# A gated scan and a top-1 mixture of experts: loads in another order, two pages with an unsplit second layer, other planning numbers

## The chip, the cores and the metric

The kernel runs on one core of one Trainium2 chip. The metric is the device time of one launch in microseconds, the median of several runs; lower is better.

## The reference

A gated linear scan along the sequence (batch 4, length 5056, width 256) gives `y`. The 20224 vectors of `y` are the tokens of a mixture of 8 experts of which each token uses one.

```python
log_a = c * sig_r * np.log(np.clip(a_base, 1e-06, 1.0 - 1e-06))   # c = 8, sig_r, sig_i: sigmoids of the gates
a_t = np.exp(log_a)
norm = np.sqrt(np.maximum(1.0 - a_t * a_t, 1e-06))
x_gated = norm * sig_i * x
for t in range(S):
    h = a_t[:, t] * h + x_gated[:, t]
    y[:, t] = h
...
logits = x @ w_gate + modality_bias[modality_id]        # x is y as 20224 x 256; 2 modalities, 8 experts
e_idx = np.argmax(logits, axis=1)
gate_w = probs[np.arange(N), e_idx]                     # softmax of the logits
for e in range(E):
    h = np.maximum(x[mask] @ w1[e], 0.0)                # mask: tokens of expert e; w1 256 x 1024
    out[mask] = gate_w[mask, None] * (h @ w2[e])        # w2 1024 x 256
```

With these inputs all but 49 tokens go to two experts (10124 and 10051 tokens).

## The kernel before

**Stages.** The sequence is cut into 23 chunks (`CHUNKS`): four of 128 time steps, seventeen of 256, one of 128 and one of 64, each for all four batches, so that a chunk has 512 or 1024 tokens. For each chunk: `load_chunk` brings `a` (the r gate), `g` (the i gate) and `x` by the queue of SyncE (SP); `scan_chunk` makes the gates on ScalarE (ACT) and VectorE (DVE) and the scan itself on DVE (L567); `size_chunk` finds a power of two for scaling; `split_chunk` writes `y` as a pair of half-precision numbers, high and low, over `a` (ACT L698, DVE L701), and TensorE (PE) makes the logits from it (L714). `route_chunk` (DVE L775 to L851, PE L816 to L819) gives each token its place in its expert's list (`di`) and moves the running totals of the experts on. `rows_part` transposes `a` into token rows `rt` (SP, L739, one transpose for 128 tokens), and GpSimd (POOL) scatters them, 128 rows at a time, into `rows` in HBM, sorted by expert (L874).

**Pages.** The sorted rows are worked off in pages of 256 tokens, in turn for the two hot experts (`HOT = 2`); later pages have 512 tokens ("wide"), and a few small pages hold the rest and the cold experts. `choose_pages` picks two pages at a time from the running totals of the chunks routed so far (`sel`, on DVE). There are two forms of this choice. For early pages, those chosen from the first `EARLY` chunks (`last`), places of the page that aren't filled yet are masked (`had`; POOL makes `hadm` and `ids` at L1167 and L1171 for the output's scatter), and a page takes whatever tokens there are. Otherwise a margin (`behind`) is kept. `load_rows` reads a page transposed from `rows` (`X`, SP, L1194) with its ids and gates (`mt`, L1195). `first_layer` multiplies X by w1 (PE L1272, 48 products for 256 tokens), `relu_pair` writes H as a high and a low half (ACT L1207, DVE L1209), `second_layer` multiplies H by w2 (PE L1432, 48 products), `layer2_tail` applies the gate (ACT L1221), and POOL scatters the result to the output (L1227). PE mixes the first layer of a page with the second layer of the page before.

**Products in half precision.** The weights of the two hot experts are loaded as fp32 (`wr0` and `wr1`: w1 and w2 of the first, `wr2` and `wr3` of the second), scaled (`scale_of`: PE L334 and L341, DVE L337), and converted into a high half (ACT L364) and a low half (DVE L370), in two steps of 1024 columns each (`hw0_0`, `hw0_1`, `hw1_0`, `hw1_1`). Every product is then three half-precision products: high by high, high by low, low by high. Between them `iv` and `hiv` carry the scales that are undone in the gate factor `gt`.

**The order of the work.** Every stage is a generator that yields an engine, a planned duration and a condition. A planner inside the kernel (`run`) takes, again and again, the one that can start first by its planned times; among those of the same engine within `WINDOW` of it, the one with the better priority (`PRIO`, four numbers for each chunk: routing, split, scan, rows; `W_AT` for the weights). `PLAN` holds its durations and due times. Thus these tables set the order in which instructions stand on each engine, and nothing else: what really waits for what on the chip is settled by semaphores. Each engine and each queue works in its order, so an instruction that waits holds up all that stand behind it. `START` is the order of the first loads; `HURRY` says for how many chunks the planner picks by a wider window; `WAIT` says how long PE may be planned to stand idle for a page before the rest of the second layer of the page before is issued alone:

```python
if queue and (prev is None or ready_at(queue[0]) < free["PE"] + WAIT):
    cur = queue.pop(0)
```

Of the kernel before, what the change touches and what calls it, by code (L numbers as in the profile page):

```python
# [17 lines left out]
P = 128  # L18
# [12 lines left out]
CHUNKS = [(128 * k, 128) for k in range(4)] + [(512 + 256 * k, 256) for k in range(17)] + [(4864, 128), (4992, 64)]  # L31
# [5 lines left out]
WAIT = 4.0  # L37
WINDOW = 0.1
# [50 lines left out]
def kernel(  # L89
# [296 lines left out]
    loads, seq = [], 0  # L386
    for what in START.split():
        if what == "w":
            what, seq = f"w{seq}", seq + 1
        loads.append(what)  # L390
    assert seq == 2 * HOT
# [12 lines left out]

    def hot_weights(m):

        e, w = m // 2, m % 2
        yield "DMA", 2.9, allof(seen(("turn", loads.index(f"w{m}") - 1)), room("wr"), lambda: 8.4), -9.0
# [91 lines left out]
    def load_chunk(c):  # L500
# [10 lines left out]
        for i, (name, src) in enumerate((("a", rs), ("g", gs), ("x", xs))):  # L511
            tag = "H" if c == 0 and name != "g" else name
            yield "DMA", 2.9 * z, room(tag), -9.0
            tickets[c, name] = tag, take(tag)
            t = (pm if tag == "H" else pa).tile([P, cols], F32, name=f"{name}{c}", tag=tag, bufs=BUFS[tag])
            LOADS.dma_start(t, src[:, base : base + cols])
            got.append(t)
# [4 lines left out]
        mark["load", c] = plan["end"]  # L522
# [877 lines left out]
    def second_layer(prev, units):  # L1400

        pg, st = prev.pg, prev.pg.st
        while units:
# [24 lines left out]
            wv = (pg.w if pg.e is None else hw[pg.e])[1].rearrange("p (s f d) -> p s f d", s=2, f=NF)  # L1428
            for _, f in run_:
                for m, (hx, wx) in enumerate(((0, 0), (0, 1), (1, 0))):  # L1430
                    prev.count += 1
                    ins = nc.tensor.matmul(  # L1432
                        prev.po, prev.h(hx, f, rs_), wv[:, wx, f], start=(prev.count == 1), stop=(prev.count == 3 * NF)
                    )
            count["pe"] = ins.ins.name
            if prev.count == 3 * NF:
# [133 lines left out]
```

## Time and profile before

| what | value |
|---|---|
| runs | 956.75, 959.58, 956.82 us; median 956.82 |
| the profiled execution | 951.06 us, span 949.1 |
| granted TensorE clock, mean | 0.983 |
| busy share of PE, DVE, ACT, POOL | 92%, 73%, 70%, 54% |
| moved by DMA | 160.95 MB, 170 GB/s over the span |
| scatters of rows (L874) and of outputs (L1227) on POOL | 158 and 160 |

Times in the profile count from the start of its span. PE is TensorE's products, PEld its weight loads (beside the products), DVE VectorE, ACT ScalarE, POOL GpSimd, SP SyncE and SPq its queue of transfers. In a row of a timeline stand the start, the duration, the engine, line and operation, the tiles written and read, the count, and in brackets how long the engine was idle before and what ended that. In a row by stretches stand the stretch, its length, the busy time and the instruction count of PE, PEld, DVE, ACT and POOL, then the granted clock of PE, the share of the transfer engines and GB/s. In a row of a group stand form, count, busy time and the mean of one in ns.

### The profile page before, as it was taken

To read this page: it belongs to the slowest core of one execution; us is meant where nothing else is said; L and a number is where in the kernel's file an instruction comes from. 1 tells how busy PE (TensorE), PEld (TensorE's weight loads), DVE (VectorE), ACT (ScalarE), POOL (GpSimd) and SP (SyncE) were. 2 spreads that over 40 slices of the span, in tenths; PEclk is the share of its full clock that TensorE was granted. 3 is DMA by queue.
4 is the path that set the end of the run, shared out by engine and by line. 5 is a ranking of instruction groups with operands and counts; after the bars stand their busy time and mean duration, and the time that the engine had idled before them with its cause. 6 is when DMAs were issued, how large, how long until landed. Compare 5 with 4: busy or idle time off the path is not lost. (4 is left out here: it accounts for less than half of the span.)

```text
span 949.1 us, 22324 instructions
## 1 busy us (share of the span) xinstructions
PE 868.8 (92%) x8485; PEld 773.5 (81%) x8485; DVE 692.1 (73%) x1526; ACT 660.2 (70%) x942; POOL 516.6 (54%) x563
## 2 busy tenths in 40 slices
PE   2286599999979999999999999999999999999996
PEld 1275578888868888888888888888888888889896
DVE  5975876877977879877788888978786667653251
ACT  7967668969967889766988879844665555554342
POOL 6424756778886868776467677755454222212212
PEclk9997899999989999999999999999999999999999
DMA  8864788878768897699698988785642222212410
GB/s 284 256 189 102 204 205 232 260 182 207 219 227 242 188 229 234 144 271 244 178 285 202 277 175 217 156 172 120 180 106 79 51 51 58 62 46 57 131 35 26
DMA packets 223334, 160.95 MB, mean 170 GB/s; under 512 B 197359, under 2 KB 202097, under 8 KB 216690
## 3 DMA queue, kind: packets, MB, share of 16 engines
q1 hardware_dynamic: 206290, 115.02, 50.2%
q0 software_dynamic: 16224, 44.25, 14.4%
q8 instruction: 68, 1.11, 0.5%
q14 instruction: 48, 0.39, 0.1%
q10 hardware_dynamic: 704, 0.18, 0.1%
HBM read 72.96 MB, written 45.01 MB: 124 GB/s over the span
## 5 line engine op out<-in xcount | busy, mean ns | idle before, releaser
L1272 PE MATMUL ph<-X,hw 128*128 128x256 f16 (+1 forms) x2880 | 355.5, 274 | 26.9 <-DMA X<-rows 24.7
L1432 PE MATMUL po<-hw,H 128*128 128x256 f16 x2832 | 349.4, 272 | 3.6 <-issue 2.1
L1272 PEld LDWEIGHTS <-hw 128*128 128x128 f16 x2880 | 277.3, 99 | 62.7 <-issue 16.2
L1432 PEld LDWEIGHTS <-H 128*128 128x128 f16 x2880 | 277.1, 98 | 36.6 <-issue 3.3
L1227 POOL DMA_INDIRECT out_dram<-ot,mt x128 | 163.9, 1281 | 218.0 <-ACT ot L1221 184.7
L874 POOL DMA_INDIRECT rows<-rt,di x158 | 208.4, 1319 | 120.8 <-issue 30.4
L1209 DVE SCALAR_TENSOR_TENSOR H<-ph,H 128x512 f16<-128x512 f32 (+1 forms) x248 | 161.6, 667 | 105.3 <-ACT H L1207 89.6
L1207 ACT ACTIVATE H<-ph 128x512 f16<-128x512 f32 (+1 forms) x248 | 141.8, 577 | 122.3 <-PE ph L1272 103.5
L1221 ACT ACTIVATE ot<-po,gt 128x256 f32<-128x256 f32 x160 | 75.2, 470 | 45.7 <-PE po L1432 35.9
L567 DVE TENSOR_TENSOR_SCAN x<-a,x 128x2048 f32<-128x2048 f32 (+2 forms) x23 | 87.9, 3821 | 0.8
L1432 PE MATMUL po<-hw,Hx 128*128 128x256 f16 x480 | 68.4, 273 | 1.2 <-ACT ot L1221 0.7
L1432 PE MATMUL po<-hw,Hg 128*128 128x256 f16 x480 | 66.9, 273 | 0.0
L1227 POOL DMA_INDIRECT out_dram<-ot,ids x32 | 54.0, 1688 | 12.6 <-issue 4.9
L553 DVE TENSOR_TENSOR x<-g,x 128x2048 f32<-128x2048 f32 (+2 forms) x23 | 45.9, 1996 | 14.0 <-ACT x L551 12.0
L701 DVE SCALAR_TENSOR_TENSOR a<-x,scy,a 128x1024 f16<-128x1024 f32 (+2 forms) x46 | 50.9, 1128 | 3.1 <-ACT a L698 3.0
L698 ACT ACTIVATE a<-x,scy 128x1024 f16<-128x1024 f32 (+2 forms) x46 | 46.0, 1020 | 9.3 <-DVE scy L306 9.0
L1432 PEld LDWEIGHTS <-Hx 128*128 128x128 f16 x480 | 46.8, 98 | 6.8 <-issue 1.5
L1362 PEld LDWEIGHTS <-sw 128*128 128x128 f16 x480 | 47.0, 98 | 5.4
L1432 PEld LDWEIGHTS <-Hg 128*128 128x128 f16 x480 | 47.0, 98 | 5.4
L544 ACT ACTIVATE a<-a,ch 128x1024 f32<-128x1024 f32 (+2 forms) x46 | 50.5, 1115 | 0.1
L539 DVE SCALAR_TENSOR_TENSOR g<-g,x 128x2048 f32<-128x2048 f32 (+2 forms) x23 | 45.7, 1988 | 2.8 <-ACT g L535 2.8
L535 ACT ACTIVATE g<-g 128x2048 f32<-128x2048 f32 (+2 forms) x23 | 38.4, 1668 | 6.9 <-DMA g<-in_i_gate_dram 6.7
(224 smaller groups left out, 1090.6 us busy)
## 6 DMA issues: line engine op xcount, KB each, us to landing
a<-in_r_gate_dram SPq DMA_DIRECT2D x17, 1024.0 KB
g<-in_i_gate_dram SPq DMA_DIRECT2D x17, 1024.0 KB
x<-in_x_dram SPq DMA_DIRECT2D x17, 1024.0 KB
wr<-in_moe_w_dram SPq DMA_DIRECT2D x4, 1024.0 KB
cr<-in_moe_w_dram SPq DMA_DIRECT2D x4, 1024.0 KB
a<-in_r_gate_dram SPq DMA_DIRECT2D x5, 512.0 KB
g<-in_i_gate_dram SPq DMA_DIRECT2D x5, 512.0 KB
x<-in_x_dram SPq DMA_DIRECT2D x5, 512.0 KB
```

What stands on the lines that cost most here:

```text
L544: nc.scalar.activation(sl, sl, AF.Exp, scale=ch[:, h : h + 1], bias=ch[:, h : h + 1])
L567: nc.vector.tensor_tensor_scan(out=y, data0=a, data1=y, initial=0.0, op0=ALU.mult, op1=ALU.add)
L698: nc.scalar.activation(ys[:, 0, :, u, :], yg[:, :, u, :], AF.Copy, scale=sc)
L701: nc.vector.scalar_tensor_tensor(out=ys[:, 1, :, u, :], in0=yg[:, :, u, :], scalar=sc, in1=ys[:, 0, :, u, :], op0=ALU.mult, op1=ALU.subtract,)
L874: ins = nc.gpsimd.indirect_dma_start(out=rows[:, :], out_offset=bass.IndirectOffsetOnAxis(ap=idx, axis=0), in_=src, in_offset=None, bounds ...
L1207: nc.scalar.activation(hi, src, AF.Relu)
L1209: nc.vector.scalar_tensor_tensor(out=lo, in0=src, scalar=0.0, in1=hi, op0=ALU.max, op1=ALU.subtract)
L1221: nc.scalar.activation(ot, po, AF.Copy, scale=t.gt[:, a : a + 1])
L1227: ins = nc.gpsimd.indirect_dma_start(out=out[:, :], out_offset=bass.IndirectOffsetOnAxis(ap=t.mt[:, a, 0:1] if t.ids is None else t.ids[:, ...
L1272: ins = nc.tensor.matmul(ph[:, v, 0:st], lhsT, rhs, start=(m == 0 and v == 0), stop=(m == len(mm) - 1), skip_group_check=True,)
L1362: ins = nc.tensor.matmul(to[:, v, :], lhsT[s], rhs[x], start=(i in (1, 7) and v == 0 and m == 0), stop=(m == 2), skip_group_check=True,)
L1432: ins = nc.tensor.matmul(prev.po, prev.h(hx, f, rs_), wv[:, wx, f], start=(prev.count == 1), stop=(prev.count == 3 * NF))
```

## The change

1. The first loads come in another order: chunk 1 before the second weight, chunk 2 before the third and fourth. (w0 to w3 are the four weight transfers.)
2. Pages 0 and 1 (`WHOLE = 2`, one page of each hot expert) keep H as one fp32 tile, written by one relu on whichever of ACT and DVE the planner has free, and their second layer is 16 fp32 products by the raw w2 of 128 tokens (32 for a page, in place of 96). The raw w2 is therefore given back only after that page, and the gate factor undoes the scale of w1 alone.
3. `EARLY` 6 to 7: pages chosen from the first seven chunks take the masked form.
4. Other numbers for the planner: `WAIT` 4 to 3, `WINDOW` 0.1 to 0.05, `HURRY` 5 to 7, `W_AT`, `PRIO` for chunks 0 to 8, and transfer and due times in `PLAN` (`dma`, `l4`, `land`, w0 to w3, `xland`, and more). `CHUNKS` has the same values as before; it is written in another way.

```diff
-START = "0 w w 1 w w 2"
+START = "0 w0 1 w1 2 w2 w3"
+WHOLE = 2
-WAIT = 4.0
-WINDOW = 0.1
+WAIT = 3.0
+WINDOW = 0.05
-W_AT = [2, 2, 6, 3]
+W_AT = [2, 2, 4, 4]
-PRIO.update({0: (6, 1, 1, 1), 1: (22, 5, 6, 9), 2: (13, 29, 20, 14), 
...
+PRIO.update({0: (1, 1, 1, 1), 1: (5, 5, 6, 1), 2: (13, 24, 15, 14), 
...
-HURRY = 5
-EARLY = 6
+HURRY = 7
+EARLY = 7
-PLAN = dict(exact=12, w0=1, w1=4, w2=8, w3=4, xland=3, row=1.55, beside=7, op=0.2, gprio=3, oh=0.3, lag=1.5, latefrom=6, 
...
+PLAN = dict(dma=3.6, l4=24, exact=12, w0=6, w1=4, w2=4, w3=3, land=0.5, xland=1.0, row=1.55, beside=9, op=0.2, gprio=3, oh=0.15, lag=1, latefrom=8, 
...
@@ hot_weights(m): e, w = m // 2, m % 2
+        raw2[e, w] = raw, tr
...
-        give("wr", tr)
+        if w == 0:
+            give("wr", tr)
         if w == 1:
...
+            yield "SP", 0.0, seen(("raw", e)), 0.0
+            give("wr", tr)
@@ layer1_tail
+        if t.whole:
+            if free["ACT"] <= free["DVE"]:
+                nc.scalar.activation(t.H[:, hs, :], ph[:, :, 0:st], AF.Relu)
+            else:
+                nc.vector.tensor_scalar(out=t.H[:, hs, :], in0=ph[:, :, 0:st], scalar1=0.0, scalar2=None, op0=ALU.max)
+            give("ph", tp)
+            return
@@ second_layer
-                    conds.append(seen(("hot", pg.e)))
+                    conds.append(seen(("got", 2 * pg.e + 1), ("w", 2 * pg.e)) if prev.whole else seen(("hot", pg.e)))
...
+            if prev.whole:
+                wv, terms = raw2[pg.e, 1][0].rearrange("p (o f d) -> p o f d", o=1, f=NF), ((0, 0),)
+            else:
+                wv = (pg.w if pg.e is None else hw[pg.e])[1].rearrange("p (s f d) -> p s f d", s=2, f=NF)
+                terms = (0, 0), (0, 1), (1, 0)
@@ expert_layers
+                cur.whole = cur.pg.n < WHOLE
```

How the order moves is seen at three places. In the names, the number after a letter is the chunk's (`a1`, `rt1`, `g5`) or the page's (`X0`, `mt0`); lines after the change are some lines further on (L519 for L516, L742 for L739, L1197 for L1194, L877 for L874, L372 for L370, L570 for L567, L1170 for L1167).

The first is the start of the pages. SP before, from chunk 3's loads to the transposes of chunk 1:

```order
L516 DMA a3_567<-in_r_gate_dram 128x1024
L516 DMA g3_598<-in_i_gate_dram 128x1024
L516 DMA x3_605<-in_x_dram 128x1024
L1189 TENSOR_LOAD sel1_613
L1189 ISA x2
L1194 ISA
L1194 DMA_TRANSPOSE X0_0_634<-rows_78 128x4x256
L1195 ISA
L1195 DMA mt0_633<-rows_78 128x2x2
```

SP after, from the same loads:

```order
L519 DMA a3_558<-in_r_gate_dram 128x1024
L519 DMA g3_583<-in_i_gate_dram 128x1024
L742 DMA_TRANSPOSE rt1_0_604<-a1_294 128x4x128 x4
L1192 TENSOR_LOAD sel1_590
L1192 ISA x2
L1197 ISA
L1197 DMA_TRANSPOSE X0_0_687<-rows_78 128x4x256
L1198 ISA
L1198 DMA mt0_686<-rows_78 128x2x2
L519 DMA x3_705<-in_x_dram 128x1024
```

The four transposes of chunk 1 have moved from behind X1 (the next page) to ahead of X0, and chunk 3's x from ahead of X0 to behind it. On DVE at the same place, ahead of chunk 1's scan, before:

```order
L370 SCALAR_TENSOR_TENSOR hw0_1_219<-wr1_294,sc1_356,hw0_1_219 128x1024
L370 SCALAR_TENSOR_TENSOR hw1_1_221<-wr3_380,sc3_455,hw1_1_221 128x1024
L424 TENSOR_TENSOR hiv0_222<-iv0_311,iv1_357 128x1
L302 TENSOR_SCALAR hsc1_225<-pt2_489 128x1
L553 TENSOR_TENSOR x1_337<-g1_331,x1_337 128x1024
L306 TENSOR_SCALAR hsc1_225<-hsc1_225 128x1
L561 TENSOR_TENSOR fed1_587<-a1_308,last0_402 128x8
L308 TENSOR_SCALAR iv2_487<-hsc1_225 128x1
L563 TENSOR_TENSOR x1_337<-x1_337,fed1_587 128x8
L370 SCALAR_TENSOR_TENSOR hw1_1_221<-wr3_380,sc3_455,hw1_1_221 128x1024
L565 MEMSET a1_308 128x8
L567 SCALAR_TENSOR_TENSOR x1_337<-a1_308,x1_337 128x1024
```

and after:

```order
L556 TENSOR_TENSOR x1_302<-g1_297,x1_302 128x1024
L308 TENSOR_SCALAR sc1_384<-sc1_384 128x1
L868 TENSOR_SCALAR sg0_497<-sg0_497,scy0_355 128x4
L870 RECIPROCAL sg0_497<-sg0_497 128x4
L564 TENSOR_TENSOR fed1_505<-a1_294,last0_358 128x8
L310 TENSOR_SCALAR iv1_385<-sc1_384 128x1
L566 TENSOR_TENSOR x1_302<-x1_302,fed1_505 128x8
L568 MEMSET a1_294 128x8
L372 SCALAR_TENSOR_TENSOR hw0_0_218<-wr0_268,hsc0_224,hw0_0_218 128x1024
L570 SCALAR_TENSOR_TENSOR x1_302<-a1_294,x1_302 128x1024
```

The weights of the second hot expert (`hw1_1`, from `wr3`) no longer stand ahead of the scan of chunk 1.

The second place is SP from chunk 4's first transposes on. Before, from there to page 7's choice:

```order
L739 DMA_TRANSPOSE rt4_0_1587<-a4_793 128x8x128 x2
L1189 TENSOR_LOAD sel4_1606
L1189 ISA x2
L1194 ISA
L1194 DMA_TRANSPOSE X6_0_1683<-rows_78 128x4x256
L1195 ISA
L1195 DMA mt6_1682<-rows_78 128x2x2
L739 DMA_TRANSPOSE rt4_0_1587<-a4_793 128x8x128 x2
L1189 TENSOR_LOAD sel4_1606
```

and after, from chunk 4's last transpose ahead of chunk 7's loads to page 8:

```order
L742 DMA_TRANSPOSE rt4_0_1702<-a4_770 128x8x128
L519 DMA a7_1939<-in_r_gate_dram 128x2048
L519 DMA g7_1992<-in_i_gate_dram 128x2048
L519 DMA x7_2056<-in_x_dram 128x2048
L742 DMA_TRANSPOSE rt5_0_2156<-a5_1056 128x8x128
L1192 TENSOR_LOAD sel5_2120
L1192 ISA x2
L1197 ISA
L1197 DMA_TRANSPOSE X8_0_2226<-rows_78 128x4x256
```

X6 stands behind two transposes of chunk 4 in both; X8 stood behind two transposes of chunk 5 before and now stands behind one.

The third place is POOL, the scatters of chunk 4's rows. Before:

```order
L752 IOTA rt4_0_1587 128x8
L758 COPY rt4_0_1587<-sg4_1745 128x8
L874 DMA rows_78<-rt4_0_1587,di4_1765 166400x258 x2
L1167 TENSOR_SCALAR hadm4_1843<-slot_195,had4_1518 128x2
L874 DMA rows_78<-rt4_0_1587,di4_1765 166400x258
L1171 TENSOR_TENSOR ids4_1842<-hadm4_1843,mt4_1531 128x2
L1227 DMA out_0_dram<-ot4_0_1729,ids4_1842 20224x256
L874 DMA rows_78<-rt4_0_1587,di4_1765 166400x258
L1227 DMA out_0_dram<-ot4_0_1729,ids4_1842 20224x256
L874 DMA rows_78<-rt4_0_1587,di4_1765 166400x258 x3
L1167 TENSOR_SCALAR hadm5_2009<-slot_195,had4_1518 128x2
L874 DMA rows_78<-rt4_0_1587,di4_1765 166400x258
```

and after:

```order
L1170 TENSOR_SCALAR hadm5_1863<-slot_195,had4_1227 128x2
L755 IOTA rt4_0_1702 128x8
L761 COPY rt4_0_1702<-sg4_1752 128x8
L877 DMA rows_78<-rt4_0_1702,di4_1793 166400x258 x8
L1174 TENSOR_TENSOR ids5_1862<-hadm5_1863,mt5_1321 128x2
L1240 DMA out_0_dram<-ot5_0_1760,ids5_1862 20224x256 x2
```

Page 4's outputs, which stood among the scatters of chunk 4, now stand ahead of them, and page 5's behind.

On PE, the second layer of a page is issued alone, with no first layer mixed in, after pages 1, 3 and 17 in the order before, and after pages 5 and 7 in the order after. All pages, products and transfers are the same in number, but for those named in points 2 and 3.

More of the change, by code (lines that the diff above doesn't have):

```diff
@@ L29 @@
 TWO23 = float(1 << 23)
-CHUNKS = [(128 * k, 128) for k in range(4)] + [(512 + 256 * k, 256) for k in range(17)] + [(4864, 128), (4992, 64)]
+RUNS = [128] * 4 + [256] * 17 + [128, 64]
+CHUNKS = [(sum(RUNS[:k]), t) for k, t in enumerate(RUNS)]
 BUFS = {
@@ L383, in convert @@
             give("dg", td)
[L386 to L391, printed above, removed]
+    loads = START.split()
     mark["turn", -1] = 0.0
@@ L403 @@
     FACTOR = (1.0, 1.0 / 1024)
+    raw2 = {}
     def hot_weights(m):
         e, w = m // 2, m % 2
-        yield "DMA", 2.9, allof(seen(("turn", loads.index(f"w{m}") - 1)), room("wr"), lambda: 8.4), -9.0
+        yield "DMA", PLAN["dma"], allof(seen(("turn", loads.index(f"w{m}") - 1)), room("wr"), lambda: 8.4), -9.0
         tr = take("wr")
@@ L512, in load_chunk @@
             tag = "H" if c == 0 and name != "g" else name
-            yield "DMA", 2.9 * z, room(tag), -9.0
+            yield "DMA", (PLAN["dma"] if c < 9 else 2.9) * z, allof(room(tag), lambda: PLAN.get(f"l{c}", 0.0)), -9.0
             tickets[c, name] = tag, take(tag)
@@ L521, in load_chunk @@
         tiles[c] = got
-        mark["load", c] = plan["end"]
+        mark["load", c] = plan["end"] + PLAN["land"]
     def done(c, name):
@@ L1413, in second_layer @@
                 if pg.e is not None and not prev.to:
-                    conds.append(seen(("hot", pg.e)))
-            yield "PE", 0.328 * len(run_), allof(*conds), 0.0
+                    conds.append(seen(("got", 2 * pg.e + 1), ("w", 2 * pg.e)) if prev.whole else seen(("hot", pg.e)))
+            yield "PE", (0.45 if prev.whole else 0.328) * len(run_), allof(*conds), 0.0
             if not prev.to:
@@ L1418, in second_layer @@
                 prev.gt = sm.tile([P, st // P], F32, name=f"gt{prev.n}", tag="gt", bufs=3)
-                nc.vector.tensor_scalar(out=prev.gt, in0=gates, scalar1=pg.inv if pg.e is None else hiv[pg.e], scalar2=None, op0=ALU.mult)
+                nc.vector.tensor_scalar(out=prev.gt, in0=gates, scalar1=pg.inv if pg.e is None else tiles["wiv", 2 * pg.e] if prev.whole else hiv[pg.e], scalar2=None, op0=ALU.mult)
             if begins:
@@ L1427, in second_layer @@
             rs_ = slice(a * P, (a + 1) * P)
-            wv = (pg.w if pg.e is None else hw[pg.e])[1].rearrange("p (s f d) -> p s f d", s=2, f=NF)
+            if prev.whole:
+                wv, terms = raw2[pg.e, 1][0].rearrange("p (o f d) -> p o f d", o=1, f=NF), ((0, 0),)
+            else:
+                wv = (pg.w if pg.e is None else hw[pg.e])[1].rearrange("p (s f d) -> p s f d", s=2, f=NF)
+                terms = (0, 0), (0, 1), (1, 0)
+            products = len(terms) * NF
             for _, f in run_:
-                for m, (hx, wx) in enumerate(((0, 0), (0, 1), (1, 0))):
+                for hx, wx in terms:
                     prev.count += 1
                     ins = nc.tensor.matmul(
-                        prev.po, prev.h(hx, f, rs_), wv[:, wx, f], start=(prev.count == 1), stop=(prev.count == 3 * NF)
+                        prev.po, prev.h(hx, f, rs_), wv[:, wx, f], start=(prev.count == 1), stop=(prev.count == products)
                     )
             count["pe"] = ins.ins.name
-            if prev.count == 3 * NF:
+            if prev.whole and prev.count == products and a == st // P - 1 and prev.pg.n >= WHOLE - HOT:
+                mark["raw", pg.e] = plan["end"]
+            if prev.count == products:
                 prev.ended[a // 2] = prev.ended.get(a // 2, 0) + 1
```

16 lines of the change are left out of this document (11 added, 5 removed).

## The prediction

> **What bounds the kernel now.** I read the page's busy times first, then the busy time of each engine by stretches, and then the tensor engine's timeline at the stretches in which it stands idle.
>
> ```profile
> span 949.1 us, 22324 instructions
> PE 868.8 (92%) x8485; PEld 773.5 (81%) x8485; DVE 692.1 (73%) x1526; ACT 660.2 (70%) x942; POOL 516.6 (54%) x563
> ...
> 51.30:76.50 25.20, 23.34 (x215) 20.04 (x214) 19.05 (x53) 16.07 (x29) 9.95 (x8) 1.00 0.54 178
> 76.50:82.80 6.30, 0.00 (x0) 0.00 (x0) 3.65 (x3) 5.87 (x5) 5.16 (x7) 0.61 0.44 113
> 82.80:107.10 24.30, 24.26 (x216) 20.77 (x217) 16.70 (x52) 15.69 (x23) 8.09 (x11) 0.89 0.81 210
> 107.10:116.80 9.70, 0.00 (x0) 0.00 (x0) 8.61 (x15) 7.50 (x6) 8.98 (x6) 0.75 0.27 66
> 116.80:162.00 45.20, 41.77 (x409) 36.08 (x409) 30.87 (x74) 29.81 (x38) 29.50 (x36) 0.94 0.86 228
> 162.00:275.90 113.90, 113.31 (x1126) 101.28 (x1124) 95.97 (x196) 97.97 (x124) 87.19 (x78) 1.00 0.81 223
> 275.90:282.00 6.10, 0.27 (x9) 0.17 (x7) 2.39 (x2) 3.67 (x3) 5.19 (x6) 0.77 0.52 136
> 282.00:600.00 318.00, 315.82 (x3174) 282.04 (x3175) 260.56 (x542) 256.75 (x334) 221.26 (x199) 0.99 0.88 220
> 600.00:941.70 341.70, 337.43 (x3232) 302.49 (x3230) 215.92 (x481) 184.42 (x334) 114.31 (x117) 1.00 0.37 89
> ```
>
> After the length of each stretch stands PE's busy time; the granted clock is third from the end. The tensor engine bounds the kernel once expert pages run: from 162 on it is busy nearly throughout. It has nothing to do for pages before 51.3, and it is empty three times, 6.3, 9.7 and 6.1 us, each time at a granted clock of 0.61 to 0.77. The change touches work from the first load to about 290 us; the order of the rest only shifts.
>
> ```profile
> 51.32 6.67 PE L1272 MATMUL ph<-X,hw 128*128 128x256 f16 x48 [2.82 <-DMA X<-rows]
> 82.83 7.96 PE L1272 MATMUL ph<-X,hw 128*128 128x256 f16 x48 [6.36 <-DMA X<-rows]
> 116.81 2.72 PE L1272 MATMUL ph<-X,hw 128*128 128x256 f16 x12 [9.72 <-DMA X<-rows]
> 160.67 1.47 PE L1432 MATMUL po<-hw,H 128*128 128x256 f16 x12
> 161.98 1.47 PE L1272 MATMUL ph<-X,hw 128*128 128x256 f16 x12
> 282.02 2.74 PE L1272 MATMUL ph<-X,hw 128*128 128x256 f16 x12 [5.85 <-DMA X<-rows]
> 284.81 2.06 PE L1272 MATMUL ph<-X,hw 128*128 128x256 f16 x12
> ```
>
> Each wait ends with a transposed page (X) that comes late: pages 0, 2, 4 and 18. At full clock twelve products take 161.98 − 160.67 = 1.31 us, 0.109 each, so a layer of a 256-token page is 5.24 us and a page 10.48. After a wait the same products are slower.
>
> **The change, part by part.** *Loads in another order; page 0.* The synchronous queue (SP) now holds X0 behind the four transposes of chunk 1's rows, which read chunk 1's split.
>
> ```profile
> 30.92 1.28 DVE L370 SCALAR_TENSOR_TENSOR hw<-wr,sc,hw 128x1024 f16<-128x1024 f32 x1
> 46.72 1.40 DVE L701 SCALAR_TENSOR_TENSOR a<-x,scy,a 128x512 f16<-128x512 f32 x2
> 48.01 1.28 SPq L1194 DMA_TRANSPOSE X<-rows  x1
> 53.05 3.83 SPq L739 DMA_TRANSPOSE rt<-a  x3
> ```
>
> In before, VectorE makes six halves of low weight parts ahead of chunk 1's scan; now two stand there and two more ahead of its split, so the split's end, 46.72 + 1.40 = 48.1, comes 4 × 1.28 = 5.1 earlier, at 43.0. Four transposes are 5.1 (3.83 for three), and from X0's issue to its first product it is 51.32 − 48.01 = 3.3: 43.0 + 5.1 + 3.3 = 51.4. With half a microsecond for queueing, I take 52.0, 0.7 later than before. The reward is that chunk 1's rows are ready at once, so page 2 no longer waits: by the prices of the chain below, 26.4 us after its split, so X2 is usable at 69.4. PE gets to page 2 after page 0's first layer (6.7), page 1's (5.2) and page 0's second (7.0 by the next part): 52.0 + 18.9 = 70.9.
>
> *Pages 0 and 1, second layer in fp32.* 96 half-precision products of 0.109 (10.5 us) become 32 fp32 ones. No row shows an fp32 product of 256 columns; the nearest fp32 rows are single columns:
>
> ```profile
> L318 PE MATMUL ptc<-ssc,onesf 128*128 128x1 f32 x8 | 1.2, 222 | 0.0
> L318 PEld LDWEIGHTS ptc<-ssc,onesf 128*128 128x128 f32 x8 | 1.2, 190 | 0.1
> L1432 PEld LDWEIGHTS <-H 128*128 128x128 f16 x2880 | 277.1, 98 | 36.6 <-issue 3.3 <-DVE H L1209 1.9
> ```
>
> The four products of L318 leave eight records, and each weight load is 190 ns against 98. Low end: two records at the half-precision price, 0.218 each, 7.0 in all (3.5 gained). High end: nothing overlaps, two loads of 190 and two double-length streams of 2 × 109, 0.816 each, 26.1 (15.6 lost). I take two double-length records with loads hidden, as loads mostly are in this trace, 0.436: 14.0, that is 3.5 lost. The Trainium skill ("FP8 and Floating Point Precision", TensorE Precision Notes) says a true fp32 product is four passes through the array; no run here shows it for 256 columns, and by it the sum would be the middle value. On VectorE and ScalarE one relu replaces a pair, and neither bounds there.
>
> *The order of chunks 1 to 5.* With all eight pages supplied in time, PE's own floor for the start of page 8 is: 52.0, eight pages of 10.48 (83.8), the fp32 surplus 3.5, page 0 at the low clock (6.67 − 5.24 = 1.4), and routing products and short waits as before: 25.20 − 23.34 = 1.9 in the first stretch and 45.20 − 41.77 = 3.4 in the fifth, 5.3. Sum 146.0. In before page 8 starts at 161.98 with page 7's second layer still to come; in the new order that layer is issued alone ahead of page 8, so the comparable time is 161.98 + 5.24 = 167.2.
>
> Whether page 8 is there at 146 is decided by chunk 4, on the chain split, routing, eight scatters, X8:
>
> ```profile
> 23.48 1.42 DVE L701 SCALAR_TENSOR_TENSOR a<-x,scy,a 128x512 f16<-128x512 f32 x2 [1.10 <-ACT a L698]
> 33.97 0.17 DVE L851 TENSOR_REDUCE b<-bh 128x2 f32<-128x16 f32 x1
> 36.35 1.30 POOL L874 DMA_INDIRECT rows<-rt,di  x1 [2.22 <-DMA rt<-a]
> 44.27 1.64 POOL L874 DMA_INDIRECT rows<-rt,di  x1 [0.30 <-issue]
> 93.80 0.42 SPq L516 DMA_DIRECT2D x<-in_x_dram  x1
> 112.16 2.48 DVE L701 SCALAR_TENSOR_TENSOR a<-x,scy,a 128x1024 f16<-128x1024 f32 x2 [0.90 <-ACT a L698]
> 114.55 2.29 DVE L539 SCALAR_TENSOR_TENSOR g<-g,x 128x2048 f32<-128x2048 f32 x1
> 136.02 4.43 DVE L567 TENSOR_TENSOR_SCAN x<-a,x 128x2048 f32<-128x2048 f32 x1
> 136.87 4.36 POOL L874 DMA_INDIRECT rows<-rt,di  x1 [0.31 <-PE ph L1272]
> 143.90 1.28 DVE L701 SCALAR_TENSOR_TENSOR a<-x,scy,a 128x1024 f16<-128x1024 f32 x1 [0.23 <-ACT a L698]
> 146.39 1.27 DVE L701 SCALAR_TENSOR_TENSOR a<-x,scy,a 128x1024 f16<-128x1024 f32 x1
> 148.91 0.99 POOL L874 DMA_INDIRECT rows<-rt,di  x1 [0.30 <-issue]
> 150.20 0.98 POOL L874 DMA_INDIRECT rows<-rt,di  x1 [0.30 <-issue]
> 158.09 1.26 SPq L1194 DMA_TRANSPOSE X<-rows  x1
> ```
>
> Chunk 0 shows the chain's prices: split end 24.9 to routing end 34.1 is 9.2, to the first scatter 2.2, four scatters 36.35 to 45.9 (9.6), then 2.1 to X0's issue at 48.01 and 3.3 to its first product: 26.4 in all from split to page.
>
> Chunk 2 feeds page 4. Its split stands on VectorE behind the relu of page 1's third quarter, which PE reaches at about 67 (70.9 less a quarter of 12.2, and a little), so it ends near 69 and X4 is usable at 95.4. PE gets there at 70.9 + 12.2 + 10.5 = 93.6, or with the routing products at 95: at most 2 us of wait remain of the 9.7.
>
>  Chunk 4 feeds page 8. Its split ended at 114.6 before; its VectorE queue loses weight work and gains chunk 5's gate product, so I leave it there. Routing then ends at 123.8, scatters begin at 126.0. Before, they were mixed with waits for output tiles and ran from 135.54 to 151.2; now the eight stand in one piece, 1.29 apart (148.91 to 150.20): 10.3, and one of them beside a scan, which costs 4.36 + 0.3 − 1.29 = 3.4. End 139.7, X8 issued 141.8, usable 145.1. But on SP one transpose of chunk 5's rows stands ahead of X8. If the first half of chunk 5's split ends as before, 143.90 + 1.28 = 145.2, X8 is usable at 145.2 + 1.3 + 3.3 = 149.8. Page 8 then starts between 146.0 and 149.8; I take 148. Gain: 167.2 − 148 = 19.2.
>
> The row of 136.87 is where a rule of the Trainium skill speaks against this: "SBUF — State Buffer" (SBUF: two separate sides) has VectorE and GpSimd lock one port pair for a whole instruction, and the other "fully blocks". The trace agrees for that scatter, 4.36 beside a scan of 4.43. By the rule chunk 5's two gate products could hold scatters in the same way, 2.3 us each by the row of 114.55, and X8 would be usable at 145.1 + 2 × 2.3 = 149.7; that lies inside my interval and moves no chance.
>
> *Page 18.* Pages 18 and 19 are now chosen from the running totals of chunk 6 instead of 7. The wait before 18 is 5.85, and 24 products run slow after it ((2.74 − 1.47) + (2.06 − 1.47) = 1.9): 7.7 gained. It adds two instructions for each of four pages to GpSimd, which is half idle. Pages 20 and 22 use the same chunks as before; page 22's choice now stands one page later on VectorE.
>
> *Moved to wide pages two pages later:* the number of wide pages is the same, so nothing is charged.
>
> **The sum.** The profiled execution took 951.06 (span 949.1 and 2 around it); 951.06 − 19.2 − 7.7 = 924.2. The runs have a median of 956.82, 5.8 above the profiled one; I subtract the same 26.9 from it: 929.9, so 930.
>
> **Rivals.** (1) Chunk 4's chain does not get shorter: page 8 comes at 158.09 + 3.3 = 161.4. For it speaks that the scatters stand behind outputs on one GpSimd queue; against it, that now only one page's outputs do. Gain 167.2 − 161.4 = 5.8, plus 7.7: 943. (2) The wait before page 18 reappears before page 20 or 22, since PE comes there 19 us earlier and chunks 7 and 8 need not. Before, page 18 alone waited in 162 to 600. Gain 19.2 only: 937.6. (3) Slower: X6 stands on SP behind chunk 4's first two transposes, and chunk 4's split stands on VectorE behind chunk 5's gate product, which needs all of chunk 5's loads. Page 6 is due on PE at about 123: 70.9, 12.2 for page 2's first layer with page 1's second, three times 10.48, the lone second layer of page 5 (5.24), and 3 of the other work. With the split at 114.6 X6 is usable near 121. Each microsecond of split beyond 117 is paid in full. If loads push it to where chunk 5's was, 146.39 + 1.27 = 147.7, X6 is usable at 147.7 + 2.6 + 3.3 = 153.6, 30.6 late; all else gained is used up, and 956.8 − 26.9 + 30.6 = 960. It decides from a split at 144 on. Against it: before, the last of chunk 5's loads was issued at 93.80 and the gate product could run at 114.55; only one stretch of 21 us lies between, so the loads have to come as early as before. (4) The waits only change places: 956.8. (5) The fp32 high end, 12.1 more than taken: page 8 at 158 to 160, gain 17, 940.
>
> **How the numbers follow.** A measurement of this kernel can tell about 0.3%, 2.9 us, from no change. Chances: forecast 0.57 (its own range 921 to 939, from the fp32 low end with X8 at 145, to a page 8 six microseconds late with part of page 18's wait left); rival 1 0.13; rival 2 0.13; rival 3 0.10; rival 4 0.04; rival 5 0.03. Faster is forecast, 1, 2 and 5: 0.86; within 0.3%: 0.04; slower: 0.10. The range from 920 to 949 takes in all but rivals 3, 4 and some hundredths.
>
> **What would show it.** Right: the first product of page 0 at 51 to 53; no idle of PE at pages 2 and 4 above 2 us; fp32 records (twice 32 for pages 0 and 1) near 220 ns apart; page 8 at 146 to 150; no empty stretch near 265. Wrong: a wait at page 6 ended by X with the transposes of chunk 4 just ahead of it on SP, a scatter row of chunk 4 waiting for VectorE, or an empty stretch at page 20 or 22.

## The result and the profile after

The changed kernel takes 925.06 us (median of 4 runs, 924.81 to 927.41), the kernel before 957.19 beside it. The ratio is 0.9665, with a 95% interval of 0.9642 to 0.9688. Forecast were 930 us and a range of 920 to 949. The profiled execution took 925.11 (span 923.3); the forecast for it was 924.2. The two medians lie 32.1 apart, the two profiled spans 25.8, since the profiled execution of the kernel before (951.06) was 6.1 under its median. The account below, like the forecast's sum, is one of the profiled executions.

The page of the changed kernel, and then its stretches. The first rows by stretches are the kernel before, cut anew: at the comparable start of page 8 (167.2, page 7's second layer then being done) and past the wait at page 18. The others are the changed kernel, cut at the same points of its work as nearly as may be.

```profile
span 923.3 us, 22274 instructions
PE 867.2 (94%) x8453; PEld 771.9 (84%) x8453; DVE 687.3 (74%) x1525; ACT 659.7 (71%) x939; POOL 514.9 (56%) x571
```

```profile
51.30:167.20 115.90, 94.57 (x887) 81.56 (x887) 82.88 (x208) 80.11 (x105) 61.67 (x65) 0.91 0.71 189
167.20:294.60 127.40, 120.97 (x1200) 107.44 (x1199) 98.52 (x197) 103.79 (x130) 99.56 (x92) 0.97 0.79 217
```

```profile
48.10:148.50 100.40, 94.67 (x853) 80.64 (x852) 80.62 (x189) 81.04 (x105) 59.60 (x70) 1.00 0.82 223
148.50:268.20 119.70, 118.83 (x1174) 106.45 (x1172) 96.98 (x196) 97.24 (x125) 84.40 (x86) 1.00 0.89 220
```

PE is busy as long as before (867.2 against 868.8); what went is idle time. From page 0 to page 8 PE works 94.6 us in both kernels and idles 21.3 before and 5.7 after. Page 0 starts 3.1 earlier. Together page 8 comes at 148.5 where 167.2 is the comparable time, 18.7 gained. From there to the end it is 949.1 − 167.2 = 781.9 before and 923.3 − 148.5 = 774.8 after, another 7.1. The sum is 25.8, the difference of the spans. The granted clock is 1.00 in both stretches, and no wait for a page above 4.4 us is left.

TensorE's timeline after:

```profile
48.18 8.73 PE L1289 MATMUL ph<-X,hw 128*128 128x256 f16 x60 [4.37 <-DMA X<-rows]
...
59.92 1.89 PE L1454 MATMUL po<-wr,H 128*128 128x256 f32 x8
61.65 1.47 PE L1289 MATMUL ph<-X,hw 128*128 128x256 f16 x12
...
143.63 0.71 PE L1454 MATMUL po<-hw,H 128*128 128x256 f16 x5 [0.84 <-issue]
145.50 0.19 PE L819 MATMUL psl<-oh,um 128*128 128x64 f16 x1 [1.17 <-DVE oh L808]
145.88 2.78 PE L1454 MATMUL po<-hw,H 128*128 128x256 f16 x24
148.50 6.71 PE L1289 MATMUL ph<-X,hw 128*128 128x256 f16 x60
```

In this trace pages 2, 4, 6 and 8 start without a wait for their X; only page 0 has one. Four fp32 products leave eight records and take 61.65 − 59.92 = 1.73 us. Page 8 starts right behind the second layer of page 7, in which PE stood a little: among its products stand the counts of chunk 5's routing, which waited for VectorE (`oh`). A row whose idle time is put down to "issue" waited for nothing that the profile shows.

The groups of fp32 records, the wait of the whole run for pages, and the chain that feeds page 8 (VectorE, GpSimd, SP):

```profile
L1454 PE MATMUL po<-wr,H 128*128 128x256 f32 x64 | 15.2, 381 | 0.0
L1454 PEld LDWEIGHTS po<-wr,H 128*128 128x128 f32 x64 | 11.5, 190 | 1.3
```

```profile
PE ph L1289 <- DMA X<-rows: 4.4, 1, 4.4
```

```profile
39.43 0.74 DVE L704 SCALAR_TENSOR_TENSOR a<-x,scy,a 128x512 f16<-128x512 f32 x1
107.11 1.27 DVE L704 SCALAR_TENSOR_TENSOR a<-x,scy,a 128x1024 f16<-128x1024 f32 x1
118.65 0.17 DVE L854 TENSOR_REDUCE b<-bh 128x2 f32<-128x16 f32 x1
130.85 2.28 DVE L542 SCALAR_TENSOR_TENSOR g<-g,x 128x2048 f32<-128x2048 f32 x1
133.99 2.47 DVE L704 SCALAR_TENSOR_TENSOR a<-x,scy,a 128x1024 f16<-128x1024 f32 x2
```

```profile
127.56 1.07 POOL L877 DMA_INDIRECT rows<-rt,di  x1 [7.50 <-PE ph L1289]
...
131.49 2.48 POOL L877 DMA_INDIRECT rows<-rt,di  x1 [0.30 <-issue]
134.28 1.82 POOL L877 DMA_INDIRECT rows<-rt,di  x1 [0.30 <-issue]
...
138.97 0.97 POOL L877 DMA_INDIRECT rows<-rt,di  x1 [0.31 <-issue]
```

```profile
43.77 1.54 SPq L1197 DMA_TRANSPOSE X<-rows  x1
...
123.54 1.24 SPq L742 DMA_TRANSPOSE rt<-a  x1
...
142.48 1.31 SPq L1197 DMA_TRANSPOSE X<-rows  x1
```

### The profile page after: what moved, and what is told of

Same layout as the page of the kernel before. It is cut to its first block, busy times and chain, and to the rows that moved or that the text cites. A ratio compares the mean times of both kernels' runs of the same rounds, so it can differ in the third digit from the quotient of the medians.

```text
span 923.3 us, 22274 instructions
## 1 busy us (share of the span) xinstructions
PE 867.2 (94%) x8453; PEld 771.9 (84%) x8453; DVE 687.3 (74%) x1525; ACT 659.7 (71%) x939; POOL 514.9 (56%) x571
## 4 chain that ended last, share of the span: by engine, by line
PE 81%; DVE 5%; issue 5%; ACT 3%; DMA 2%; POOL 2%; another core or an unknown queue 1%; SPq 1%; POOLq 0%; ACTq 0%; DVEq 0%
PE po L1454 40%; PE ph L1289 30%; PE pb L1379 4%; PE pc L1379 3%; PE pa L1379 3%; POOL out_dram L1240 1%; PE psl L717 1%; DMA wr<-in_moe_w_dram 1%; DVE H L1212 1%; ACT H L1210 0%; DMA X<-rows 0%; DMA wg<-in_moe_w_gate_dram 0%; ACT g L584 0%; DVE a L704 0%
## 5 line engine op out<-in xcount | busy, mean ns | idle before, releaser
L1289 PE MATMUL ph<-X,hw 128*128 128x256 f16 (+1 forms) x2880 | 349.3, 272 | 6.1 <-DMA X<-rows 4.4
L1454 PE MATMUL po<-hw,H 128*128 128x256 f16 x2736 | 339.3, 272 | 6.3 <-issue 3.1
L1454 PEld LDWEIGHTS <-H 128*128 128x128 f16 x2784 | 266.6, 98 | 40.5 <-issue 7.0
L877 POOL DMA_INDIRECT rows<-rt,di x158 | 223.1, 1412 | 113.2 <-PE po L1454 28.5
L1240 POOL DMA_INDIRECT out_dram<-ot,mt x120 | 142.6, 1189 | 193.9 <-ACT ot L1234 163.4
L1212 DVE SCALAR_TENSOR_TENSOR H<-ph,H 128x512 f16<-128x512 f32 (+1 forms) x240 | 156.1, 664 | 68.6 <-ACT H L1210 53.8
L1210 ACT ACTIVATE H<-ph 128x512 f16<-128x512 f32 (+1 forms) x240 | 138.0, 578 | 89.7 <-PE ph L1289 58.1
L570 DVE TENSOR_TENSOR_SCAN x<-a,x 128x2048 f32<-128x2048 f32 (+2 forms) x23 | 87.8, 3818 | 0.6
L1240 POOL DMA_INDIRECT out_dram<-ot,ids x40 | 61.0, 1524 | 36.1 <-ACT ot L1234 12.9
L1210 ACT ACTIVATE Hg<-sv 128x512 f16<-128x512 f32 x40 | 25.0, 626 | 22.6 <-DVE sv L1327 22.2
```

The lines of the kernel that those rows point to most:

```text
L570: nc.vector.tensor_tensor_scan(out=y, data0=a, data1=y, initial=0.0, op0=ALU.mult, op1=ALU.add)
L877: ins = nc.gpsimd.indirect_dma_start(out=rows[:, :], out_offset=bass.IndirectOffsetOnAxis(ap=idx, axis=0), in_=src, in_offset=None, bounds ...
L1210: nc.scalar.activation(hi, src, AF.Relu)
L1212: nc.vector.scalar_tensor_tensor(out=lo, in0=src, scalar=0.0, in1=hi, op0=ALU.max, op1=ALU.subtract)
L1240: ins = nc.gpsimd.indirect_dma_start(out=out[:, :], out_offset=bass.IndirectOffsetOnAxis(ap=t.mt[:, a, 0:1] if t.ids is None else t.ids[:, ...
L1289: ins = nc.tensor.matmul(ph[:, v, 0:st], lhsT, rhs, start=(m == 0 and v == 0), stop=(m == len(mm) - 1), skip_group_check=True,)
```

## The experiments

Chips differ. The kernel before had medians of 957.2, 956.3, 946.6 and 945.9 us on the four chips used. So every run is read by its ratio to the kernel before on its own chip; the expectations, which name times on the first, are to be scaled. The table gives them in one place; the changed kernel has 0.9665 on the first chip and 0.9707 on the fourth. It was not run on the second and third, so what an edit of it costs there is given by both ratios.

| kernel | chip | median us | ratio to before | 95% interval |
|---|---|---|---|---|
| changed, EARLY 6 | second | 937.89 | 0.9815 | 0.9778 to 0.9853 |
| before, EARLY 7 | second | 943.17 | 0.9874 | 0.9834 to 0.9914 |
| changed, fp32 products twice | second | 939.65 | 0.9824 | 0.9782 to 0.9867 |
| changed, half of the fp32 products | second | 923.26 | 0.9664 | 0.9627 to 0.9700 |
| changed, WHOLE 0 | third | 947.34 | 1.0008 | 0.9992 to 1.0023 |
| changed, loads as before | third | 926.12 | 0.9780 | 0.9745 to 0.9814 |
| changed, priorities as before | third | 929.82 | 0.9830 | 0.9801 to 0.9859 |
| changed, planned times as before | third | 925.30 | 0.9780 | 0.9736 to 0.9823 |
| changed, again | fourth | 918.65 | 0.9707 | 0.9670 to 0.9743 |
| before, fp32 pages added | fourth | 936.78 | 0.9899 | 0.9858 to 0.9939 |
| before, loads in the new order | fourth | 927.54 | 0.9799 | 0.9765 to 0.9832 |

**The masked choice for pages 18 and 19, alone and taken out.**

```diff
# on the kernel before
-EARLY = 6
+EARLY = 7
```

> The kernel before with EARLY 7 in place of 6, nothing else. If the masked choice is worth the whole wait at page 18 by itself: 957 - 7 = 950, PE's idle time at page 18 gone, pages 0 to 16 as before. Rival: the wait only moves to page 20 or 22, since the chunks aren't earlier: within 2 us of 957.

Measured 0.9874, 12 us less (8 to 16 by the interval; 7.1 by the spans of the profiled executions, 949.1 and 942.0, on different chips). The waits for pages of the whole run (sum, number, longest), in the kernel before and after this edit alone:

```profile
PE ph L1272 <- DMA X<-rows: 24.7, 4, 9.7
PE ph L1272 <- DMA X<-rows: 20.0, 3, 9.8
```

Three waits are left of four: those at pages 0, 2 and 4. The wait at page 18 is gone and has not come back at 20 or 22. So the first theory holds, with a gain at or above the 7 that was named; what is above it is not placed.

```diff
# on the changed kernel
-EARLY = 7
+EARLY = 6
```

> The changed kernel with EARLY back at 6, so that pages 18 and 19 are chosen from chunk 7 with a margin. If the masked choice is what removed the wait at page 18, that wait is back at page 18, 5 to 8 us of idle time and slow products, and the time is about 932 (925 + 7). Rival: page 18 no longer waits because the earlier work (chunk 7 done sooner in the new order) has removed it anyway; then PE has no gap at page 18 and the time stays within 2 us of 925.

Measured 0.9815, 10 to 14 us above the changed kernel by its two ratios. The time goes the first theory's way, and further, but the place is another: page 18 does not wait. The waits of the run for pages, and TensorE's timeline at its end:

```profile
PE ph L1289 <- DMA X<-rows: 3.4, 1, 3.4
```

```profile
915.58 0.38 PE L320 MATMUL ptc<-ssc,onesf 128*128 128x1 f32 x2 [2.50 <-ACT cw L316]
920.57 0.59 PE L320 MATMUL ptc<-ssc,onesf 128*128 128x1 f32 x2 [4.61 <-ACT cw L316]
```

The only wait for a page is page 0's. The loss stands at the very end: the planner has put the scaling of the last cold expert's weights (`cw`) behind the last page's work, where PE waits for it; in the changed kernel the same work runs beside products (PE L320 at 897.18 and 905.93, no wait). The first products of the last small page then start at 921.02, and at 909.71 in the changed kernel. So the rival was right on page 18: in the new order it has no wait to remove. The total pointed to the first theory by another cause.

**The price of the fp32 products, with all instructions in their places.**

```diff
-                wv, terms = ..., ((0, 0),)
+                wv, terms = ..., ((0, 0), (0, 0))
```

> The changed kernel with each fp32 product of pages 0 and 1 issued twice (32 more fp32 products; the second layer of these two pages comes out doubled). All instructions stand in the same places. If PE bounds the stretch from page 0 to page 8, the time grows by the products' own time, 32 x 0.433 = 13.9 us: 939. Rival: the pages' arrival bounds it (chunk 2, 3 and 4's chains), and PE has slack that takes up most of the addition: 925 to 932.

Measured 0.9824. 956.3 × (0.9824 − 0.9665) = 15.2 us more, or 11.2 by the changed kernel's other ratio, where 13.9 were expected of a stretch that PE bounds. In the trace the stretch from page 0 to page 8 grows from 100.3 to 116.0 us (50.01 to 165.99). Added products are paid in full, within these errors.

```diff
             products = len(terms) * (NF // 2 if prev.whole else NF)
             for _, f in run_:
+                if prev.whole and f % 2:
+                    continue
```

> The changed kernel with every second fp32 product of pages 0 and 1 left out (half of the hidden width missing in these two pages). All else stands in the same places. If PE bounds the stretch, 16 x 0.433 = 6.9 us less: 918. Rival: the arrival of pages 4 to 8 bounds it and PE waits instead: 923 to 925, with waits for X at page 4, 6 or 8 in place of the products.

Measured 0.9664: no gain by the first chip's ratio, 4.1 us by the fourth's, where 6.9 were expected of PE's bound. The time is the rival's, but its mechanism is seen only in part. Between 66 and 91 PE waits 3.6 us that it does not wait there in the changed kernel, for work on the chunks by VectorE (1.6) and ScalarE (1.4), and for page 4's X (0.6). The rest is lost ahead of page 8:

```profile
141.57 0.27 PE L1456 MATMUL po<-hw,H 128*128 128x256 f16 x1 [0.22 <-issue]
142.28 0.61 PE L1456 MATMUL po<-hw,H 128*128 128x256 f16 x4 [0.44 <-issue]
143.70 1.44 PE L1456 MATMUL po<-hw,H 128*128 128x256 f16 x6 [0.81 <-issue]
146.24 0.21 PE L819 MATMUL psl<-oh,um 128*128 128x64 f16 x1 [1.10 <-DVE oh L808]
146.64 4.49 PE L1456 MATMUL po<-hw,H 128*128 128x256 f16 x24
150.96 6.71 PE L1289 MATMUL ph<-X,hw 128*128 128x256 f16 x60
```

Page 8's first product stands at 150.96, 2.5 later than in the changed kernel although PE had less to do. Ahead of it stand the second layer of page 7 in pieces, its last 24 products at 4.49 us in place of 2.78, and chunk 5's counts, which wait for VectorE as in the changed kernel. Page 8 does not wait for its X: X8 was issued at 142.75, and by the 3.2 us from issue to product that the fourth chip's trace shows below it was usable near 146. So this run does not show that the arrival of pages is the limit. What holds the pieces of page 7's second layer the trace does not name ("issue").

**The order of the loads, alone and taken out.**

```diff
# on the kernel before
-START = "0 w w 1 w w 2"
+START = "0 w 1 w 2 w w"
```

> The kernel before with only the loads in the new order (chunk 0, w0, chunk 1, w1, chunk 2, w2, w3). If the loads' order by itself brings chunks 1 and 2 earlier, one of the waits at pages 2 and 4 goes: 940 to 950 where the kernel before takes 957. Rival: priorities keep VectorE in the old order and the chunks that land earlier lie about: within 3 us of the kernel before.

Measured 0.9799 on the chip on which the changed kernel had 0.9707: 18.3 of 27.2 us by one line, the first theory and a little more. TensorE's longest waits in it:

```profile
48.61 2.72 PE L1272 MATMUL ph<-X,hw 128*128 128x256 f16 x12 [6.19 <-DMA X<-rows]
87.14 2.72 PE L1272 MATMUL ph<-X,hw 128*128 128x256 f16 x12 [5.10 <-DMA X<-rows]
265.57 1.48 PE L1272 MATMUL ph<-X,hw 128*128 128x256 f16 x12 [3.01 <-DMA X<-rows]
```

The wait at page 2 is still there (5.1), that of 9.7 at page 4 has no successor above 2 us, and that at page 18 is 3.0 with products at full clock behind it. All waits for pages are 16.6 us here and 27.7 in the kernel before on the same chip, and PE's busy time is 862.0 against 868.1: these two differences, 11.1 and 6.1, come to the 17.2 us between the two spans (947.0 and 929.8). PE's other idle time changes by under 1 us in sum.

```diff
# on the changed kernel
-START = "0 w0 1 w1 2 w2 w3"
+START = "0 w0 w1 1 w2 w3 2"
```

> The changed kernel with the loads in the order of before (chunk 0, w0, w1, chunk 1, w2, w3, chunk 2). Chunk 1 lands one weight transfer later (about 4 us) and chunk 2 two (about 7). If the order of the loads carries the early arrival of pages 2 and 4, PE waits there again, 4 to 12 us: 929 to 937. Rival: the priorities carry it, and the loads have slack: within 3 us of 925.

Measured 0.9780, 7 to 11 us above the changed kernel by its two ratios, with four waits for pages of 7.5 us in all; the longest are 3.4 at page 2 and 2.7 at page 8, and page 4 has none. That fits the first theory in size; of the two places it names, page 2 waits and page 4 does not.

**The priorities, and the planned times.**

```diff
-W_AT = [2, 2, 4, 4]
+W_AT = [2, 2, 6, 3]
-PRIO.update({0: (1, 1, 1, 1), 1: (5, 5, 6, 1), ...})
+PRIO.update({0: (6, 1, 1, 1), 1: (22, 5, 6, 9), ...})
```

> The changed kernel with the priorities of before (PRIO for chunks 0 to 8 and W_AT), the rest as in the change. If the priorities set when chunks 1 to 4 are split and scattered, the waits at pages 2 and 4 come back with low clock, some 19 us: 940 to 944. Rival: the loads' order and the transfer times in PLAN do most, and the time is 925 to 932.

Measured 0.9830, 12 to 16 us above the changed kernel's ratios. The five waits for pages are 13.9 us in all, with these two the longest:

```profile
50.08 4.34 PE L1289 MATMUL ph<-X,hw 128*128 128x256 f16 x24 [5.17 <-DMA X<-rows]
123.32 2.74 PE L1289 MATMUL ph<-X,hw 128*128 128x256 f16 x12 [4.75 <-DMA X<-rows]
```

By size that is at the lower edge of the first theory (0.9830 of 957 is 941), but not in the place named: page 0 waits 5.2 (4.4 in the changed kernel) and page 6 4.8, page 4 only 0.9 and page 2 not at all.

```diff
-PLAN = dict(dma=3.6, l4=24, ...)
+PLAN = dict(dma=2.9, land=0, ...)   # all others as before
```

> The changed kernel with the planner's durations and due times of before (PLAN, transfers at 2.9), the rest as in the change. Planned times alone differ, so the order differs where two threads are close. If the planned times are as important as the priorities: 930 to 944, with waits for X in the first eight pages. Rival: they only fine-tune: 922 to 929.

Measured 0.9780 (0.9736 to 0.9823), 7 to 11 us above the changed kernel; seven small waits, the longest 2.4. The run's own time, 925.3, lies in the rival's range, but on a chip on which the kernel before is 10 us faster; by ratio the planned times do seem to matter, though the interval touches that of the changed kernel on the fourth chip (0.9670 to 0.9743).

**The fp32 pages, alone and taken out.**

```diff
# on the kernel before, with its START, PRIO, PLAN and EARLY
+WHOLE = 2
```

> All tables of before (loads, priorities, planned times, EARLY 6), with only the fp32 second layer of pages 0 and 1 added; the planner orders anew, and X2 then stands on SP behind chunk 2's and half of chunk 3's transposes. If the fp32 pages by themselves bring the pages earlier, the waits at pages 2 and 4 shrink: 935 to 945. Rival: they need the new tables; alone they add 3.4 us of products and page 2 waits for chunk 2's and 3's splits: 955 to 975.

Measured 0.9899, 9 us faster, which is 947 on the first chip's scale: between the two ranges, just short of the first. PE's longest waits:

```profile
91.85 8.32 PE L1289 MATMUL ph<-X,hw 128*128 128x256 f16 x49 [9.17 <-DMA X<-rows]
268.69 2.74 PE L1289 MATMUL ph<-X,hw 128*128 128x256 f16 x12 [5.11 <-DMA X<-rows]
```

Page 2 now waits for 9.2 us, since X2 stands behind chunk 3's transposes as expected. The wait at page 18 is there as before (5.1). But the wait at page 4 is no more, and the sum comes out lower: 17.2 us, where the kernel before has 27.7 on the same chip.

```diff
-WHOLE = 2
+WHOLE = 0
@@ hot_weights(m)
-            yield "SP", 0.0, seen(("raw", e)), 0.0
+            if WHOLE: yield "SP", 0.0, seen(("raw", e)), 0.0
```

> The changed kernel with WHOLE 0: pages 0 and 1 in half precision like all others, all tables as in the change (the planner then orders the start anew). If the fp32 products are only a cost, PE has 64 half-precision products more and 32 fp32 ones less, 10.5 - 13.9 = -3.4 us: 921.5. Rival: what the fp32 pages buy is that VectorE has 8 relu instructions of 0.67 us less and that w2's conversion is off the path, so that chunks 2 to 4 come earlier; without it pages 4 to 8 wait, 4 to 10 us: 929 to 935.

Measured 1.0008, as slow as the kernel before. Neither theory: the tables are fitted to two fp32 pages, and without them the planner makes another order, with waits at pages 4 and 12

```profile
118.17 9.34 PE L1289 MATMUL ph<-X,hw 128*128 128x256 f16 x60 [5.99 <-DMA X<-rows]
214.68 8.89 PE L1289 MATMUL ph<-X,hw 128*128 128x256 f16 x60 [5.32 <-DMA X<-rows]
```

and 74 pages in place of 72 (by the gate factors `gt`, one for each page). So this run tells nothing of the fp32 products' own price; the doubled ones do.

**Both kernels again.**

> The changed kernel once more, beside the kernel before on the same chip. The kernel before had medians of 956 to 957 us on the first two chips and 946.6 on the third. If the difference comes from the kernel before alone (its waits for pages vary from chip to chip, the changed kernel has few), the changed kernel comes at 925 (within 2) here too, whatever the kernel before takes. Rival: the chip moves both, and the ratio stays near 0.967.

Measured 918.65 beside 945.85, 0.9707 (0.9670 to 0.9743). The rival: the chip moves both kernels, and the two intervals of the ratio overlap. The trace is not the same as on the first chip:

```profile
121.85 6.72 PE L1289 MATMUL ph<-X,hw 128*128 128x256 f16 x60 [1.62 <-DMA X<-rows]
141.14 2.78 PE L1454 MATMUL po<-hw,H 128*128 128x256 f16 x24
144.34 1.27 SPq L1197 DMA_TRANSPOSE X<-rows  x1
147.58 8.39 PE L1289 MATMUL ph<-X,hw 128*128 128x256 f16 x60 [3.66 <-DMA X<-rows]
```

Page 7's second layer runs here without the pieces and is done at 143.9. Then PE waits 3.7 us for X8, which was issued at 144.34 and used 3.2 later. So here the arrival sets the start of page 8, at 147.6, and page 6 waits 1.6 as well.

> The kernel before once more, for its profile on this chip. If its waits vary, the idle time before pages 2, 4 and 18 and the low clock behind them differ from 6.4, 9.7 and 5.9 us, and the rest of the time agrees within 2 us.

One execution, 948.97. The waits at pages 2, 4 and 18 are 6.05, 9.64 and 5.78, the same within 0.4 us as on the first chip, and one at page 8 has come:

```profile
161.27 1.71 PE L1272 MATMUL ph<-X,hw 128*128 128x256 f16 x12 [3.93 <-DMA X<-rows]
```

So these three waits are alike in the two traces, and the difference between chips is not in them. With the changed kernel's trace from the same chip the span falls by 30.7 us: 18.9 up to page 8 (161.27 + 5.24 against 147.58) and 11.8 after it.

What does differ between chips is idle time ended by nothing that the profile shows ("issue", or "remote" on VectorE). In the six traces from the first two chips TensorE has 4.3 to 6.4 us of it and VectorE 20 to 44; in the eight from the third and fourth TensorE has none and VectorE at most 4.2. Two of these groups in the first trace of the changed kernel:

```profile
PE po L1454 <- issue: 3.1, 8, 0.8
DVE H L1212 <- issue: 9.5, 9, 2.2
```

The slower two chips are those with this idle time, but no run shows what it is or how much of their 10 us it makes; the cause stays open. Open too is why the first profiled execution of the kernel before (951.06) lies 5.8 under its median.

## Why the prediction was right, point by point

| term | predicted | measured |
|---|---|---|
| first product of page 0 | 52.0 | 48.2 |
| an fp32 product of 256 columns | 0.436 | 0.433 |
| page 0 to page 8 on PE | 94.0 | 100.3 |
| chunk 4's split ends | 114.6 | 108.4 |
| its scatters begin, end | 126.0, 139.7 | 127.6, 139.9 |
| X8 issued | 141.8 | 142.5 |
| first product of page 8 | 148 | 148.5 |
| gain up to page 8 | 19.2 | 18.7 |
| gain after it (page 18) | 7.7 | 7.1 |
| profiled execution | 924.2 | 925.1 |

The forecast of 930 took the same 26.9 off the median of the kernel before. Between the medians the gain was 32.1, 5.2 more, and no term of the sum stands for that.

*Page 0* came 3.8 early, outside the 51 to 53 that I named as a sign. The step that was off is the end of chunk 1's split: I only subtracted the four weight rows that had left VectorE's queue, 43.0. It ended at 39.43 + 0.74 = 40.2, which is 2.8 of the 3.8. The scan of chunk 1 stands at 32.25 after and at 39.60 before, 7.3 earlier, of which four rows are 5.1. Chunk 1's loads now stand ahead of w1, and I had put the order of the loads at nothing there. The rest is that X0 was issued 3.6 after the split, not 5.1 and a half, and used 4.4 after its issue, not 3.3.

*PE's floor* was 6 too small for this trace. 83.8 of page products, 3.4 of fp32 surplus (32 × 0.433 − 10.5) and 5.7 of idle time leave 7.4. 2.0 of them are the first 60 products, which take 8.6 us instead of 6.5 (I had 1.4). The other 5 are logit and routing products, which I had in the sum as idle time only and not as work, and slowed pieces around 112 and 143. But on the fourth chip, without these pieces, PE gets from page 0 to the end of page 7 in 143.9 − 48.1 = 95.8, 1.8 more than said. So most of the 6 are the pieces, which I did not foresee and no run explains. On the first chip they happen to cancel page 0's early start; on the fourth X8's arrival does, 3.7 after PE is ready. That page 8 came at 148 on the first chip is luck in part: the pieces took the place of a wait for X8, which by the same 3.2 was usable near 145.7.

*The fp32 products* take 0.433 each, four times a half-precision product of 0.109. My middle value was 0.436. The Trainium skill's four passes ("FP8 and Floating Point Precision", TensorE Precision Notes) agree with the trace. The loads of 190 ns are hidden: 64 of them would be 12 us by themselves, and PE shows no idle time for them.

*Chunk 4's chain* ended where I put it, by two errors that cancel, and that is luck: its split came 6.2 early, and its first scatter began 8.7 after the routing's end (118.8) instead of 2.2. The trace names a product as the releaser of the scatter's 7.5 us of idle time. But SP's last transpose of chunk 4 was issued at 123.54, behind X7, and the scatter began 4.0 later. It does so in the second trace of the changed kernel (124.59, 128.61; 5.3 later with halved products) and with doubled products, where this transpose is the releaser that is named:

```profile
138.94 1.23 SPq L742 DMA_TRANSPOSE rt<-a  x1
142.95 1.29 POOL L877 DMA_INDIRECT rows<-rt,di  x1 [6.55 <-DMA rt<-a]
```

So the step that was off is that chunk 4's last transpose stands behind X7 on SP's queue, which the chain from routing to scatters left out. The interval in which I put page 8, between PE's floor and X8's arrival, was right in kind: the doubled products cost their full price, and the fourth chip's trace shows the wait for X8. The halved products are no clean test of it.

*GpSimd beside VectorE.* I charged one scatter held for 3.4 us by a scan. Two were held, for 1.5 and 0.9 us more than the usual 0.97, beside chunk 6's gate product (130.85, 2.28 us) and chunk 5's split (133.99, 2.47 us for two halves), 2.4 in all. That is what the Trainium skill's rule ("SBUF — State Buffer", SBUF: two separate sides) would have for products of two inputs: the trace agrees with it here. Chunk 5's two gate products ran earlier, at 102.38 and 119.95, and chunk 5's scan at 122.59 was done before the first scatter.

*Page 18* gained 7.1 where 7.7 was said, but the reason I gave was only one of two. The masked choice removes that wait in the old order (EARLY 7 alone). In the new one it would not have come back (EARLY 6): the earlier chunks suffice. There the masked choice instead changes the work at the end of the run. So the size came out right by a reason that was not mine.

*The rivals.* Chunk 4's chain did shorten (rival 1), no wait appeared at pages 20 or 22 (rival 2), chunk 5's gate product stood ahead of chunk 4's split without delaying X6 (rival 3: issued at 116.81, used at 122.54 with no wait for it, and with one of 1.6 on the fourth chip). The waits did not only change places, 24.7 us of them became 4.4 (rival 4), and the fp32 high end is out (rival 5).

What I did not see is how the gain divides. By the medians, the loads' order alone brings 18.3 us, the fp32 pages 9.1 and EARLY 13.1; together they would make 40, and the change has 27 to 32. In part they remove the same waits: the loads' order and the fp32 pages both that at page 4, the loads' order and EARLY that at page 18, the first by half. What the priorities and the planned times bring alone was not run. Taking any one part out of the change costs 0.7 to 3.5% by the changed kernel's two ratios; since the planner then makes another order, this is not the part's own worth.

## What to carry to other kernels

When an engine is fed by a chain of stages, write down its own floor, small products included, and the chain's arrival as two separate times and forecast between them. Doubling the engine's work in place tests the one side; a second trace of the same kernel, on another chip, can show which idle pieces belong to the order and which do not, as page 8 shows here. In a kernel that is ordered by a planner, undoing one number makes a new order: find where the time went in that run's trace before its total is taken as evidence, as the kernel with EARLY 6 shows, whose total pointed to the wrong theory.

## What the runs showed of the hardware that was not expected

The same kernel differs by 1.2% from chip to chip (945.9 to 957.2 us), with the same three longest waits for pages in its traces; the ratio of the two kernels differed by 0.4% between two chips (0.9665 and 0.9707). Idle time that the profile gives no cause for stood on VectorE for 20 to 44 us in every trace of two chips and for at most 4.2 in every trace of the other two. An fp32 product of 128 x 128 by 256 columns costs 0.433 us with its two 190 ns weight loads hidden, so that a layer in fp32 with unsplit weights costs only a third more than the three half-precision products that it replaces (13.9 against 10.5 us for two pages), and needs one relu in place of a pair.
